# Three reorderings in an attention, MoE and MLP kernel: float64 steps, one expert's sums, and low halves

## The chip, the cores and the metric

The program runs on one core of one Trainium2 chip. Times are device microseconds (us) of one execution. Inputs and outputs are those of the reference; w_in and w_out arrive as float64 and are cut to pairs of float16 by the kernel itself. Below, PE is the matmul engine (PEld its weight loads), DVE the vector engine, ACT the scalar engine, POOL the GpSimd engine and SP the engine that issues the transfers. Each engine works through its own list of instructions in order and waits at an instruction whose inputs or buffers are not ready.

## The reference, cut to what matters

```python
x = attention(q, k, v)                    # (1152, 512): a pooled and a local softmax attention, added
P = sinkhorn(exp(x @ w_gate))             # (1152, 8)
out = 0
for e in range(8):                        # MoE: every token goes through every expert
    h = np.maximum(x @ w1[e], 0.0)        # (1152, 1024)
    out += P[:, e:e + 1] * (h @ w2[e])
h = out @ w_in                            # MoE2: (1152, 2048)
sp = np.where(h > 20.0, h, np.log1p(np.exp(np.minimum(h, 20.0))))
return (h * np.tanh(sp)) @ w_out
```

## The kernel before, in words

Every matrix that goes into a product is split into a float16 high half and a float16 low half, so that a product is three matmuls (high x high, high x low, low x high). The order of the instructions is written out by hand: the Python code issues the products, and between them it calls `tick()`, which takes one step (up to a `yield`) from each of the queues `first` and `second`, and one from `spare` where `more` is true. What a step issues goes to the end of each engine's list at that moment.

**Experts.** Expert 0 is done product by product (L1019), with its second products (`G2`, L1174) at 142 to 175 us. For experts 1 to 7, `G1_7` does the first products with seven block products instead of eight (`SEVEN`). `ORDER7` lists them: 56 words and two dashes, n = 0 to 57, and "2M7" is product M7 of output group 2. A word is six matmuls of 288 columns (L1143). Behind each product stands what empties its bank: ACT copies it out (`snap`, L1105, for M1, M6 and M5; L1160 for M3), or DVE adds it to such a copy (`add`, L1109, for M2, M7 and M4). PE's banks for these products are rings: M7 and M4 share the two banks of ring Z, so that 2M7 (n = 22) must wait until the DVE add of 0M4 (n = 18) is done, 3M7 (n = 24) for that of 1M4 (n = 20), and 4M7 (n = 33) for that of 2M4 (n = 29). M1, M6, M5 and M3 of a group add up in one bank of ring X, so that 4M5 (n = 30) waits for ACT's copy of 4M6 (n = 25), and 0M3 (n = 15) for that of 0M5. Three words after a group's last add ACT writes the ReLU (L1117, "h"), and three words later DVE its low half (L1118, "low").

**Steps beside the first products.** `tick` is called at every odd n and at multiples of 8. `second` carries the split of this expert's w2: four squares for its scale on ACT (L267), then four high parts on ACT (L243, "W") and four low parts on DVE (L256, "wbl"). `spare` carries `Split64.gen`, which turns w_in and w_out into float16 pairs and stores them to DRAM: per piece clamp and shift (DVE L429, L431), join of bits (DVE L434, L436), a square and the next piece's magnitude (ACT L443, L416, on which the next L429 waits), sums and differences of blocks (DVE L487, L534), scaling (ACT L528), and cuts for the store (ACT L492 then DVE L497; ACT L469 then DVE L470). In `G1_7` this queue gets a step where `more` is true, at n = 15, 19, 23, ... 55; in `G2` it gets 24 steps per expert, as it does after the change. It starts near the end of expert 1's first products.

**Sums of W1 of expert 1.** `early_gen` forms three sums of blocks of W1[1] on DVE (L290), their high halves on ACT (L293) and their low halves on DVE (L296), in steps between the last first products of expert 0 (whose results go through ACT L1028, ACT L637 and DVE L1037) and the start of `G2` of expert 0.

**MoE2.** A first product (`First`) goes through `N1` in half steps, i even and i odd, with four of them in flight: a (newest), b, d, e (oldest). `third` and `fourth`, `second2` hold DVE adds that empty PE's banks (L1660), `sums` is one ACT and four DVE instructions (L1663, L1713), `high` one on ACT (L1719), `low` one on DVE (L1722). Half steps alternate with eight-product units of `G2` or of the second products (L1783).

Of the kernel before, what the change touches and what calls it, by code (L numbers as in the profile page):

```python
# [21 lines left out]
def attn_moe_moe2_kernel(ctx: ExitStack, tc: tile.TileContext, q, k, v, w_gate, w1, w2, w_in, w_out, out):  # L22
# [73 lines left out]
    def all_max(m, tag="ma"):  # L96
        ma = sm.tile([128, 1], F32, tag=tag, name=tag)
        nc.gpsimd.partition_all_reduce(ma, m, 128, RED.max)  # L98
        return ma
# [17 lines left out]
    class Steps:  # L117
# [8 lines left out]
        def tick(self, n=1):  # L126
            while n > 0 and self.q:
                try:
                    next(self.q[0])
                    n -= 1  # L130
                except StopIteration:
                    self.q.pop(0)
            return n
# [5 lines left out]
    first, second, spare = Steps(), Steps(), Steps()  # L139
# [139 lines left out]
    class SplitSums(SplitSq):  # L279
# [4 lines left out]
        def early_gen(self, part, halves):  # L284

            (a11, a21), (a12, a22) = [[halves(r)[:, :, n * 512:(n + 1) * 512] for n in range(2)] for r in self.raw]
            s = halves(late["ws"].tile([128, 1024], F32, tag="ws", name="ws"))

            def tt(out, u, v, op):
                nc.vector.tensor_tensor(out=out, in0=u, in1=v, op=op)  # L290

            def hi(n, src):
                nc.scalar.activation(out=halves(part(0, n)), in_=src, func=AF.Copy, scale=self.s)  # L293

            def lo(n, src):
                nc.vector.scalar_tensor_tensor(out=halves(part(1, n)), in0=src, scalar=self.s, in1=halves(part(0, n)),  # L296
                                               op0=ALU.mult, op1=ALU.subtract)

            tt(s, a11, a21, ALU.subtract)
            hi(S3_, s)  # L300
            yield
            tt(a21, a21, a22, ALU.add)
            yield
            lo(S3_, s)
            tt(s, a21, a11, ALU.subtract)
            hi(S2_, s)
            yield
            yield
            lo(S2_, s)
            tt(s, a12, s, ALU.subtract)  # L310
            hi(S4_, s)
            yield
            yield
            lo(S4_, s)
            while not self.free:
                yield
            self.tiles()
            last = None
            for n, src in ((A11_, a11), (A12_, a12), (A22_, a22), (S1_, a21)):
                hi(n, src)  # L320
                yield
                if last:
                    lo(*last)
                yield
                last = n, src
            lo(*last)
            yield
# [59 lines left out]
    class Split64:  # L387
# [21 lines left out]
        def gen(self):  # L409
            for i in range(3):  # L410
                self.fetch(i)

            def magnitude(i):

                w = self.w32()
                nc.scalar.activation(out=w, in_=self.words[i][:, :, 1].bitcast(F32), func=AF.Abs)  # L416
                return w

            last, prev = None, None
            for _ in range(4):  # L420
                yield
            nxt = magnitude(0)
            yield
            for i, (src, f) in enumerate(self.todo):
                w = nxt
                wi = w.bitcast(I32)
                lo, hi = self.words[i][:, :, 0], self.words[i][:, :, 1]

                nc.vector.tensor_scalar(out=w, in0=w, scalar1=LOW, scalar2=HIGH, op0=ALU.max, op1=ALU.min)  # L429

                nc.vector.tensor_scalar(out=wi, in0=wi, scalar1=3, scalar2=2 ** 30 - 1, op0=ALU.logical_shift_left,  # L431
                                        op1=ALU.bitwise_and)
                yield
                nc.vector.scalar_tensor_tensor(out=wi, in0=lo, scalar=29, in1=wi, op0=ALU.logical_shift_right,  # L434
                                               op1=ALU.bitwise_or)
                nc.vector.scalar_tensor_tensor(out=wi, in0=hi, scalar=-2 ** 30, in1=wi, op0=ALU.bitwise_and,  # L436
                                               op1=ALU.bitwise_or)
                self.fetch(i + 3)
                yield
                if f < 8:  # L440
                    mq = sm.tile([128, 2], F32, tag="m6", name="m6")
                b = cvp[0].tile([128, CW], BF16, tag="junk", name="junk", bufs=1)
                nc.scalar.activation(out=b, in_=w, func=AF.Square, accum_out=mq[:, f // 8:f // 8 + 1])  # L443
                if i + 1 < len(self.todo):
                    nxt = magnitude(i + 1)
                if f >= 8:
                    yield
                    m1 = sm.tile([128, 1], F32, tag="m7", name="m7")
                    nc.vector.tensor_tensor(out=m1, in0=mq[:, 0:1], in1=mq[:, 1:2], op=ALU.add)
                    if not src:  # L450
                        m1 = all_max(m1, "ma6")
                    yield
                if last:
                    yield from self.parts_in(*last)
                    last = None
                if f < 8:
                    prev = w
                elif src == 0:
                    last = f - 8, prev, w, m1
                else:  # L460
                    yield from self.parts_out(f - 8, prev, w, m1)
# [626 lines left out]
    def G1_7(w, h, fill):  # L1088
# [32 lines left out]
        def due(n):  # L1121
            lows.sort(key=lambda x: x[0])
            while lows and lows[0][0] <= n:
                lows.pop(0)[1]()

        for n, word in enumerate(ORDER7.split()):
# [3 lines left out]
            else:  # L1130
                gi, m = item
                b, f = gi // 4, gi % 4
                g = open_.setdefault(gi, {})
                a, bn, bank, before = SEVEN[m]
# [30 lines left out]
                    parts(n, b, f + 4, g["r2"])  # L1165
            due(n)
            if n % 2 or n % 8 == 0:
                tick(more=n > 12 and n % 4 == 3)
        due(1000)

    def G2_products(ps, w, h, t, ft):
# [119 lines left out]
    with tc.manual_schedule():  # L1291
# [437 lines left out]
        def N1(c, i, more=True):  # L1729

            if i % 2 == 0:
                if more:
                    n = 8 * c + i // 2
                    for k in range(2):
                        win_load(k, n + 2)
                    firsts.append(First(c, i // 2))
                    firsts[-1].begin()
                else:  # L1740
                    firsts.append(None)
                firsts.pop(0)
            a, b, d, e = firsts[::-1]
            if i % 2 == 0:
                for it, step in ((b, "third"), (a, "begin2"), (d, "sums"), (e, "low")):
                    if it:
                        getattr(it, step)()
            else:
                for it, step in ((a, "second"), (b, "fourth"), (a, "second2"), (d, "high")):
                    if it:  # L1750
                        getattr(it, step)()

# [74 lines left out]
        e = E - 1  # L1827
# [28 lines left out]
        n = [0]  # L1856
# [27 lines left out]
        for c in range(NC2):  # L1884
            n = [0]
# [49 lines left out]
```

## Time and profile before

| | |
|---|---|
| three runs, us | 986.39 median (982.49 to 990.14) |
| profiled execution, us | 983.91 |
| its span, us | 982.1 |
| granted clock of PE, mean | 0.998 of full speed |
| busy share of the span | PE 97%, PEld 66%, DVE 73%, ACT 58%, POOL 7% |
| DMA queue 1 | 122.59 MB, 39.9% of 16 engines' span |

The table's shares are means over the whole program. Attention fills the first 75 us or so, expert 0 ends at 175 us, the first products of experts 1 to 7 begin at about 175, 264, 356, 445, 533, 624 and 712 us and take some 43 us each, the rest of each expert is second products, and MoE2 takes the time from 776 us on.

### The profile page before, as it was taken

Reading aid. Unit: us, or ns where it says so; the run is one execution under the profiler, and the core shown is the slowest. Engines: PE = TensorE matmul, PEld = TensorE weight load, DVE = VectorE, ACT = ScalarE, POOL = GpSimd, SP = SyncE. Lnnn points to the kernel's source line nnn. Section 1 sums busy time; section 2 is a strip of 40 time slices with the busy share of each in tenths; the row PEclk is TensorE's granted clock in tenths of the full one; section 3 lists DMA queues with packets and bytes.
Section 4 is the critical chain, followed back from the end, with each engine's and each line's share of the span. In section 5 each row is a group of like instructions: output and inputs, shape, how many; then the busy total and the mean of one; then the engine's idle time right before and its main releaser. Section 6 shows DMA issues by size and latency. Waiting matters only on the chain. (4 is left out here: it accounts for less than half of the span.)

```text
span 982.1 us, 20942 instructions
## 1 busy us (share of the span) xinstructions
PE 952.6 (97%) x8501; PEld 652.6 (66%) x8504; DVE 716.4 (73%) x1507; ACT 568.2 (58%) x1162; POOL 64.2 (7%) x116
## 2 busy tenths in 40 slices
PE   6899998999999999999999999999999999999998
PEld 5676674774566467547745764674476577999997
DVE  5887578679577949794996789498858467877741
ACT  4776344766376457747763774577375265665631
POOL 5524100000000000000000000000000000000000
PEclk9999999999999999999999999999999999999999
DMA  9863202022413242242424232332303756767781
GB/s 212 166 147 109 90 1 86 1 86 72 161 66 111 69 157 84 106 139 70 151 81 150 87 107 87 134 134 65 124 1 108 288 185 203 264 206 208 224 269 36
DMA packets 97707, 123.91 MB, mean 126 GB/s; under 512 B 36812, under 2 KB 72012, under 8 KB 96588
## 3 DMA queue, kind: packets, MB, share of 16 engines
q1 hardware_dynamic: 97612, 122.59, 39.9%
q8 instruction: 66, 1.08, 0.5%
q14 instruction: 29, 0.24, 0.1%
HBM read 104.48 MB, written 18.09 MB: 125 GB/s over the span
## 5 line engine op out<-in xcount | busy, mean ns | idle before, releaser
L1174 PE MATMUL mm<-wbh,h 128*128 128x512 f16 x1152 | 352.4, 379 | 2.5 <-ACT h L637 2.4
L1174 PEld LDWEIGHTS <-h 128*128 128x128 f16 x1728 | 167.6, 98 | 194.9 <-ACT h L637 2.9
L1174 PE MATMUL mm<-wbl,h 128*128 128x512 f16 x576 | 218.3, 379 | 0.0
L1109 DVE SCALAR_TENSOR_TENSOR r<-mm,s 128x288 f32<-128x288 f32 x168 | 75.5, 455 | 78.3 <-PE mm L1143 73.7
L1143 PE MATMUL mm<-x,wah 128*128 128x288 f16 x672 | 128.8, 287 | 0.0
L1143 PEld LDWEIGHTS <-wx 128*128 128x128 f16 x1008 | 98.9, 98 | 34.0 <-issue 8.9
L1143 PEld LDWEIGHTS <-wah 128*128 128x128 f16 x896 | 88.0, 98 | 27.3 <-issue 1.0
L1143 PE MATMUL mm<-xt,wx 128*128 128x288 f16 x672 | 97.0, 286 | 7.6 <-DVE r L1109 7.6
L1105 ACT ACTIVATE s<-mm 128x288 f32<-128x288 f32 x168 | 66.5, 411 | 61.4 <-PE mm L1143 61.0
L1649 PEld LDWEIGHTS <-win 128*128 128x128 f16 x1536 | 92.3, 98 | 10.2 <-issue 3.9
L1143 PE MATMUL mm<-x,wal 128*128 128x288 f16 x336 | 96.6, 287 | 0.0
L1118 DVE SCALAR_TENSOR_TENSOR h<-r,h 128x576 f16<-128x576 f32 x112 | 81.6, 750 | 0.0
L1117 ACT ACTIVATE h<-r 128x576 f16<-128x576 f32 x112 | 74.3, 680 | 9.4 <-DVE r L1109 9.1
L443 ACT ACTIVATE junk<-w 128x512 bf16<-128x512 f32 x32 | 20.1, 627 | 76.6 <-DVE w L436 74.1
L1207 DVE SCALAR_TENSOR_TENSOR acc<-mm,pc,acc 128x512 f32<-128x512 f32 x63 | 46.8, 746 | 19.6 <-PE mm L1174 19.6
L1656 ACT ACTIVATE s<-mm 128x128 f32<-128x128 f32 x96 | 26.6, 277 | 57.0 <-PE mm L1649 55.6
L98 POOL PARTITION_ALL_REDUCE ma<-m x25 | 14.1, 563 | 670.2 <-DVE m L271 395.6
L1649 PE MATMUL mm<-xc,win 128*128 128x128 f16 x864 | 56.1, 219 | 1.2 <-DVE acc L1207 0.7
L267 ACT ACTIVATE junk<-raw 128x1024 bf16<-128x1024 f32 x52 | 54.9, 1056 | 0.2
L1143 PEld LDWEIGHTS <-wal 128*128 128x128 f16 x448 | 43.9, 98 | 11.2
L1143 PE MATMUL mm<-x,wx 128*128 128x288 f16 x336 | 51.1, 289 | 0.0
L1660 DVE TENSOR_TENSOR tt<-mm,s 128x128 f32<-128x128 f32 x96 | 24.8, 285 | 34.2 <-ACT s L1656 31.9
(287 smaller groups left out, 1543.0 us busy)
## 6 DMA issues: line engine op xcount, KB each, us to landing
raw<-in_moe_w_dram SPq DMA_DIRECT2D x44, 512.0 KB, 4.8
win<-scri SPq DMA_DIRECT2D x40, 512.0 KB, 4.6
win<-scri SPq DMA_DIRECT2D x40, 384.0 KB, 3.7
raw<-in_moe_w_dram SPq DMA_DIRECT2D x10, 1024.0 KB, 5.9
f<-in_moe_w_in_dram SPq DMA_DIRECT2D x16, 512.0 KB, 3.7
f<-in_moe_w_out_dram SPq DMA_DIRECT2D x16, 512.0 KB, 3.6
scr<-st SPq DMA_DIRECT2D x32, 256.0 KB, 2.6
scri<-st SPq DMA_DIRECT2D x56, 128.0 KB, 1.9
```

Of the source, the lines that this page charges most:

```text
L267: nc.scalar.activation(out=junk, in_=r[:, c * 1024:(c + 1) * 1024], func=AF.Square, accum_out=mx[:, 2 * i + c:2 * i + c + 1])
L443: nc.scalar.activation(out=b, in_=w, func=AF.Square, accum_out=mq[:, f // 8:f // 8 + 1])
L1105: nc.scalar.activation(out=t, in_=ps, func=AF.Copy, scale=HSC)
L1109: nc.vector.scalar_tensor_tensor(out=out, in0=ps, scalar=HSC, in1=r, op0=ALU.mult, op1=ALU.add)
L1117: lows.append((n + 3, lambda: nc.scalar.activation(out=hi, in_=r, func=AF.Relu)))
L1118: lows.append((n + 6, lambda: nc.vector.scalar_tensor_tensor(out=lo, in0=r, scalar=0.0, in1=hi, op0=ALU.max, op1=ALU.subtract)))
L1143: nc.tensor.matmul(ps, lhsT=w.part(wi, a)[:, c:c + 128], rhs=factor(b, bn, xi, i), start=(not before and k == 0), stop=(k == 5), skip_grou ...
L1174: nc.tensor.matmul(ps, lhsT=h[ft][:, hi, t * 128:(t + 1) * 128], rhs=wt[:, ws], start=(ft == 0 and n == 0), stop=(ft == FT - 1 and n == 2))
L1207: nc.vector.scalar_tensor_tensor(out=a, in0=ps, scalar=pc[:, t:t + 1], in1=a, op0=ALU.mult, op1=ALU.add)
L1649: nc.tensor.matmul(self.bank(bank), lhsT=self.win[i][:, n, wi, kk * 128:(kk + 1) * 128], rhs=self.x[:, xi, xn, kk * 128:(kk + 1) * 128], s ...
L1656: nc.scalar.activation(out=t, in_=self.ps[:, 0], func=AF.Copy)
L1660: nc.vector.tensor_tensor(out=self.tt[:, o], in0=self.bank(bank), in1=r, op=ALU.add)
```

## The change

Three edits of order; no instruction of the computation is added or taken away.

```diff
@@ early_gen (sums of W1 of expert 1)
             tt(s, a11, a21, ALU.subtract)
+            yield
             hi(S3_, s)
-            yield
             tt(a21, a21, a22, ALU.add)
             yield
             lo(S3_, s)
             tt(s, a21, a11, ALU.subtract)
+            yield
             hi(S2_, s)
-            yield
             yield
             lo(S2_, s)
             tt(s, a12, s, ALU.subtract)
+            yield
             hi(S4_, s)
-            yield
             yield
             lo(S4_, s)
@@ Split64.gen
             last, prev = None, None
-            for _ in range(4):
+            for _ in range(3):
                 yield
@@ G1_7
             if n % 2 or n % 8 == 0:
-                tick(more=n > 12 and n % 4 == 3)
+                tick(more=n % 2 and (n < 24 and n % 6 != 1 or n > 44 and n % 4 == 3))
@@ N1
             if i % 2 == 0:
-                for it, step in ((b, "third"), (a, "begin2"), (d, "sums"), (e, "low")):
+                for it, step in ((b, "third"), (a, "begin2"), (d, "sums")):
                     if it:
                         getattr(it, step)()
             else:
-                for it, step in ((a, "second"), (b, "fourth"), (a, "second2"), (d, "high")):
+                for it, step in ((a, "second"), (b, "fourth"), (a, "second2"), (d, "high"), (e, "low")):
```

In `early_gen` each high half goes to ACT one step after the DVE instruction that forms its input, and no longer in the same step. In `G1_7` the float64 queue still gets 11 steps per expert, now at n = 3, 5, 9, 11, 15, 17, 21 and 23 and then at 47, 51 and 55: none at 25 to 45. In expert 1 the queue starts too late for the early ones; it stands two steps further back from there on, and its last step still falls into expert 7's first products. In `N1` the low half of the oldest product is cut at the end of the odd half step, behind that half step's adds, and no longer at the end of the even one. PE's list of instructions is the same before and after, apart from the numbers of buffers.

Three places of the order, as it stood and as it stands. The first is ACT's list at the end of expert 0's first products: L1028 takes a product of expert 0 out of its bank, L637 makes its high half, and L293 is a high half of a sum of W1[1], whose input `ws` or `raw` DVE forms. Before:

```order
L1028 ACTIVATE r<-mm_2583 128x288
L293 ACTIVATE wx<-ws,sc_w_1_2200 128x1024
L1028 ACTIVATE r<-mm_2605 128x288
L637 ACTIVATE h<-r 128x576
L1028 ACTIVATE r<-mm_2632 128x288
L293 ACTIVATE wx<-ws,sc_w_1_2200 128x1024
L1028 ACTIVATE r<-mm_2650 128x288
L637 ACTIVATE h<-r 128x576
L293 ACTIVATE wx<-ws,sc_w_1_2200 128x1024
L293 ACTIVATE wah<-raw,sc_w_1_2200 128x1024
```

After:

```order
L1028 ACTIVATE r<-mm_2583 128x288
L1028 ACTIVATE r<-mm_2604 128x288
L637 ACTIVATE h<-r 128x576
L293 ACTIVATE wx<-ws,sc_w_1_2200 128x1024
L1028 ACTIVATE r<-mm_2632 128x288
L1028 ACTIVATE r<-mm_2649 128x288
L637 ACTIVATE h<-r 128x576
L293 ACTIVATE wx<-ws,sc_w_1_2200 128x1024 x2
```

Each of the three L293 on `ws` has moved behind the next L1028 and L637 of expert 0. DVE's list is the same in this stretch.

The second place is DVE's list in the first products of expert 7, from the add of 1M4 (n = 20) on: L1109 are the adds of 1M4, 2M7 (n = 22), 3M7 (n = 24) and 3M2 (n = 27) in this order, L534 and L470 are float64 steps. Before:

```order
L1109 SCALAR_TENSOR_TENSOR r<-mm_8748,s_8688 128x288
L1118 SCALAR_TENSOR_TENSOR h<-r,h 128x576
L1109 SCALAR_TENSOR_TENSOR r<-mm_8839,s_8763 128x288
L1118 SCALAR_TENSOR_TENSOR h<-r,h 128x576
L256 SCALAR_TENSOR_TENSOR wbl<-raw,sc_w_7_8772,wbh 128x1024
L534 TENSOR_TENSOR w_8859<-w_8400 128x256
L534 TENSOR_TENSOR w_8859<-w_8467,w_8859 128x256
L1109 SCALAR_TENSOR_TENSOR r<-mm_8862,s_8854 128x288
L1118 SCALAR_TENSOR_TENSOR h<-r,h 128x576
L256 SCALAR_TENSOR_TENSOR wbl<-raw,sc_w_7_8772,wbh 128x1024
L1118 SCALAR_TENSOR_TENSOR h<-r,h 128x576
L1109 SCALAR_TENSOR_TENSOR r<-mm_8893,s_8670 128x288
```

After:

```order
L1109 SCALAR_TENSOR_TENSOR r<-mm_8753,s_8686 128x288
L1118 SCALAR_TENSOR_TENSOR h<-r,h 128x576
L470 TENSOR_TENSOR st<-w_8447,st 128x2x256
L1109 SCALAR_TENSOR_TENSOR r<-mm_8846,s_8768 128x288
L1118 SCALAR_TENSOR_TENSOR h<-r,h 128x576
L256 SCALAR_TENSOR_TENSOR wbl<-raw,sc_w_7_8777,wbh 128x1024
L534 TENSOR_TENSOR w_8447<-w_8489,w_8804 128x256
L534 TENSOR_TENSOR w_8447<-w_8489,w_8447 128x256
L470 TENSOR_TENSOR st<-w_8489,st 128x2x256
L1109 SCALAR_TENSOR_TENSOR r<-mm_8872,s_8861 128x288
```

The cut L470, which stood behind the add of 3M2, now stands ahead of the add of 2M7, a second one ahead of the add of 3M7; from there to the add of 3M4 (n = 31) no float64 row is left.

The third place is DVE's list in MoE2 beside the transposition of the second chunk (L1568, L1570, L1572, L1573) and the end of a tile of second products (L1207). Before:

```order
L1713 TENSOR_TENSOR tt<-tt 128x128 x4
L1722 SCALAR_TENSOR_TENSOR g<-tt,cf_9343,g 128x896
L1568 SCALAR_TENSOR_TENSOR xb<-mm_9714,xcs_9494,xa 128x256
L1570 TENSOR_SCALAR xb<-mm_9714,xcs_9494 128x256
L1207 SCALAR_TENSOR_TENSOR acc<-mm_9547,pc_9176,acc 128x512
L1660 TENSOR_TENSOR tt<-mm_9598,s_9647 128x128
L1660 TENSOR_TENSOR tt<-mm_9677,s_9691 128x128
L1572 TENSOR_TENSOR xb<-xb 128x256
```

After:

```order
L1713 TENSOR_TENSOR tt<-tt 128x128 x4
L1568 SCALAR_TENSOR_TENSOR xb<-mm_9713,xcs_9494,xa 128x256
L1570 TENSOR_SCALAR xb<-mm_9713,xcs_9494 128x256
L1207 SCALAR_TENSOR_TENSOR acc<-mm_9547,pc_9176,acc 128x512
L1660 TENSOR_TENSOR tt<-mm_9598,s_9646 128x128
L1660 TENSOR_TENSOR tt<-mm_9677,s_9691 128x128
L1722 SCALAR_TENSOR_TENSOR g<-tt,cf_9343,g 128x896
L1572 TENSOR_TENSOR xb<-xb 128x256
```

The low half L1722 has moved from ahead of the adds L1660 to behind them.

## Rows read from the trace of the kernel before

**Rows 1.** The page, busy us of each engine, share of the span, instructions

```profile
PE 952.6 (97%) x8501; PEld 652.6 (66%) x8504; DVE 716.4 (73%) x1507; ACT 568.2 (58%) x1162; POOL 64.2 (7%) x116
```

**Rows 2.** PE's waits: engine, tile, line, releaser: us in total, times, longest us

```profile
PE mm L1143 <- DVE r L1109: 7.6, 7, 2.3
...
PE mm L1174 <- ACT h L637: 2.4, 1, 2.4
PE mm L1649 <- DVE tt L1660: 1.9, 3, 0.8
...
PE mm L1649 <- DVE acc L1207: 0.7, 1, 0.7
PE cp L1284 <- DVE cs L1279: 0.7, 1, 0.7
...
PE mm L1143 <- ACT s L1105: 0.4, 2, 0.2
```

**Rows 3.** Timeline of PE, products 4M7: start, us, instruction, [idle before]

```profile
290.63 0.90 PE L1143 MATMUL mm<-xt,wx 128*128 128x288 f16 x6 [2.28 <-DVE r L1109]
...
737.73 0.90 PE L1143 MATMUL mm<-xt,wx 128*128 128x288 f16 x6 [0.64 <-DVE r L1109]
...
739.19 0.90 PE L1143 MATMUL mm<-x,wx 128*128 128x288 f16 x6
```

**Rows 4.** Windows: us, PE, PEld, DVE, ACT, POOL busy, clock, DMA, GB/s

```profile
292.00:294.00 2.00, 2.00 (x11) 1.28 (x9) 2.00 (x5) 1.03 (x3) 0.00 (x0) 0.50 1.06 370
294.00:296.00 2.00, 2.00 (x13) 1.37 (x12) 2.00 (x5) 0.76 (x2) 0.45 (x1) 0.67 0.99 383
150.00:155.00 5.00, 4.16 (x21) 1.86 (x20) 4.79 (x10) 2.01 (x2) 0.00 (x0) 1.00 0.00 0
```

**Rows 5.** Timeline of ACT, then PE, at the sums of W1[1]

```profile
147.55 1.15 ACT L293 ACTIVATE wx<-ws,sc_w 128x1024 f16<-128x1024 f32 x1 [5.61 <-DVE ws L290]
...
149.76 0.39 PE L1174 MATMUL mm<-wbh,h 128*128 128x512 f16 x1 [2.36 <-ACT h L637]
```

**Rows 6.** Timeline of DVE in the first products of expert 7

```profile
729.55 0.46 DVE L1109 SCALAR_TENSOR_TENSOR r<-mm,s 128x288 f32<-128x288 f32 x1 [0.35 <-PE mm L1143]
...
731.89 0.42 DVE L534 TENSOR_TENSOR w<-w 128x256 f32<-128x256 f32 x1
...
732.69 0.45 DVE L1109 SCALAR_TENSOR_TENSOR r<-mm,s 128x288 f32<-128x288 f32 x1
...
736.62 0.69 DVE L470 TENSOR_TENSOR st<-w,st 128x512 f16<-128x512 f32 x1
737.22 0.45 DVE L1109 SCALAR_TENSOR_TENSOR r<-mm,s 128x288 f32<-128x288 f32 x1
```

**Rows 7.** Timelines of ACT and DVE in expert 4, of ACT in expert 7

```profile
462.48 1.14 ACT L243 ACTIVATE wbh<-raw,sc_w 128x1024 f16<-128x1024 f32 x1
...
464.38 1.32 ACT L528 ACTIVATE w<-w,s_out 128x512 f32<-128x512 f32 x2
...
464.57 0.45 DVE L1109 SCALAR_TENSOR_TENSOR r<-mm,s 128x288 f32<-128x288 f32 x1
...
730.75 1.14 ACT L243 ACTIVATE wbh<-raw,sc_w 128x1024 f16<-128x1024 f32 x1
...
735.89 0.64 ACT L469 ACTIVATE st<-w 128x512 f16<-128x512 f32 x1
```

**Rows 8.** Timeline of DVE in the first products of expert 2

```profile
284.06 0.43 DVE L429 TENSOR_SCALAR w<-w 128x512 f32<-128x512 f32 x1 [1.03 <-ACT w L416]
...
284.86 0.45 DVE L1109 SCALAR_TENSOR_TENSOR r<-mm,s 128x288 f32<-128x288 f32 x1
```

**Rows 9.** Groups by line: count | busy us, mean ns | idle before

```profile
L434 DVE SCALAR_TENSOR_TENSOR w<-f,w 128x512 int32<-128x512 int32 x32 | 22.0, 687 | 0.3
```

**Rows 10.** Timeline of DVE, then PE, in MoE2

```profile
823.90 1.15 DVE L1722 SCALAR_TENSOR_TENSOR g<-tt,cf,g 128x896 f16<-128x896 f32 x1
...
826.87 0.83 PE L1649 MATMUL mm<-xd,win 128*128 128x128 f16 x12 [0.81 <-DVE tt L1660]
```

## The prediction

> **What bounds the kernel now.** I read the busy shares first: PE is busy for 97% of the span and DVE for 73% [rows 1]. A change of order on DVE and ACT can therefore gain only where PE stands still, so I read the list of PE's waits next. Those that the three edits can reach are few: 7.6 us in seven waits of first products for a DVE add (L1109) and 0.4 us for ACT copies, 2.4 us in one wait of expert 0's second products for a high half (L637), 0.7 us of a copy that feeds the next one, 1.9 us in three waits of MoE2 for the adds L1660, and 0.7 us for L1207 [rows 2]. Together that is 13.7 us of 982.1. The timeline of PE says where: the long waits of the experts all stand at the product 4M7, 2.28 us in expert 2 and 0.64 us in expert 7 [rows 3]. Last I read the clock. After the 2.28 us wait it is 0.50 for one window of 2 us and 0.67 for the next [rows 4], which costs (1 - 0.50) x 2 + (1 - 0.67) x 2 = 1.66 us on top. So the three edits play for 15.4 us at most.
>
> **Edit 1, sums of W1[1].** ACT came to L293 at 147.55 - 5.61 = 141.94 and waited there for a DVE sum [rows 5]. Behind it in the same list stood L1028 and L637, which PE needed, so PE waited 2.36 us at 149.76. After the edit L1028 and L637 stand ahead of that L293, and their input is a finished product. Those 2.4 us go. Of the 0.7 us of the copy L1284, whose input comes from the same crowded stretch of DVE, I take 0.4, since DVE's list there does not change (bounds 0 and 0.7). What becomes late is the split of W1[1], by one step; PE's first use of it is at 175 us. Edit 1: **-2.8** (-2.4 to -3.1).
>
> **Edit 2, the float64 steps.** No instruction is removed. Steps leave n = 25 to 45, where they stood ahead of the adds that 4M7 needs, and go to n = 3 to 23, where most adds are not waited for. With a product every 0.73 us (739.19 - 737.73 is two of them [rows 3]) I walked through each expert's lists as they will stand. In expert 7 the spare of DVE ahead of 4M7 can be read: two L534 and an L470 stand there, 2 x 0.42 + 0.69 = 1.53 us [rows 6], and PE waits 0.64, so about 0.9 us of foreign work fits for nothing.
>
> Expert 7: the cut L470 that now stands ahead of the add of 2M7 needs ACT's L469, which stands right behind ACT's second W. That W began at 730.75; L528 (1.3 us) no longer stands between the first and the second W, so W begins earlier, though by about 1.0 only, since the copy ahead of it then waits for its product. W takes 1.14 and L469 0.64 [rows 7]: L469 ends near 731.4 and L470 near 732.0, where the add of 2M7 stood at 729.55. From there to the add of 2M4 DVE has the same rows as before (two L534, one L470) and had no idle time, so the lateness of 2.45 reaches 4M7: 2.45 + 0.64 = 3.1, part of it shown at 3M4.
>
> Expert 4: L528 now stands ahead of the second W, and L469 and L470 come at n = 23. From W's start to L528's start is 1.90 in the rows, W with a copy and a ReLU row. So W begins at 462.48 + 1.32, L469 at 465.70, L470 at 466.34 and the add of 3M7 at 467.0, where it stood at 464.57 [rows 7]: 2.5 late, less the two L534 (0.84) that no longer follow it, 1.6 at 4M7.
>
> Expert 2: before, L429 waited 1.03 us for ACT's magnitude L416, the add behind it stood still until 284.86 [rows 8], and that made the 2.28 us. The same step now comes at n = 17, ahead of the add of 0M4, for which 2M7 waits. Ahead of that magnitude ACT has a W (1.14 alone, 1.90 with a copy and a ReLU row [rows 7]), then the square and the magnitude (about 1.3, an estimate from the L528 pair, as large), and L429 and L431 take 0.80 (284.06 to 284.86): the add starts 3.2 to 4.0 us after product 17 ends, where 0.7 would do. It may be 1.7 late for nothing (three products of 0.73, less 0.51 from add to PE, 737.22 to 737.73 [rows 3, 6]), so 2M7 waits 0.8 to 1.6; I take 1.2 (outer bounds 0 and 2.3, the whole of the old wait). At n = 21 L434 and L436 (2 x 0.69 [rows 9]) add 1.4 - 0.9 = 0.5 at 4M7.
>
> Experts 3, 5 and 6 have such a pair at n = 15 to 23 too: 0.5 each at 4M7, and 0.3 in all for 0M3, which waits for ACT copies while steps crowd ACT at n = 3 to 15. Expert 1 keeps its 0.2. Sum after: 3.1 + 1.6 + 1.7 + 1.8 + 0.2 = 8.4, against 7.6 + 0.4 before: **+0.4** (bounds -7.8 with no hold at all, +10.8 with all six like expert 7).
>
> [...] Without any such hold in experts 2, 4 and 7, edit 2 would give -4.9 and not +0.4.
>
> The clock: the 2.28 us wait lost 1.66 us, but the clock is 1.00 from 150 to 155 us although a 2.36 us wait stood in front [rows 4, 5]. Expert 7's wait, split in two, may do either. I count half: **-0.8** (0 and -1.7).
>
> [...] The two waits of this trace, alike in length, ended at 0.50 and at 1.00. By the one the forecast is 0.8 higher, by the other 0.8 lower.
>
> The transfers of the moved steps (fetch and store of a piece on SP) move with them, and this expert's weight loads stand behind them; no wait of PE in the list is for a transfer, and the pieces are all stored by the end of expert 7's first products, as before. I cost that at nothing; a weight quarter that came late would cost PE its wait directly.
>
> **Edit 3, low halves.** Before 826.87 DVE cut a low half (L1722, 1.15 us) at 823.90, and then the adds L1660 came, for which PE waited 0.81 [rows 10]. With the low half behind them these 0.81 go, and so does one more of the three, whose adds also have a low half and nothing that waits for PE ahead (0.55, half of the 1.1 that is left of 1.9). The third, and L1207's 0.7, wait for a row that is itself waiting for PE, so nothing is gained there. The low half is used by second products half a step or more later. **-1.4** (0 to -2.6).
>
> **Sum.** -2.8 + 0.4 - 0.8 - 1.4 = -4.6. The profiled execution took 983.9, so 979.3; the runs' median is 986.4, 2.5 above it, and against that I forecast **981.8**.
>
> **The rivals.** (a) All waits go, as the places of the steps suggest: nothing at n = 25 to 45, so 4M7 waits nowhere. For it: the waits before are behind such steps. Against it: experts 2, 4 and 7 as walked through. All 13.7 + 1.7 = 15.4 go: **971.0**. (b) The holds are more than I found: two more experts hold as expert 4 does (1.6 with a clock drop of 1.7, for 0.5 each), and no drop is saved. 981.8 + 2 x 2.8 + 0.8 = **988.2**, no change. For it: ACT gets two steps more before n = 24 beside squares, W and copies; against it: most of those steps have their inputs ready by a word or two. (c) Slower: in each of the six experts 2 to 7 DVE stands behind ACT as in expert 7, 3.1 + 1.7 of clock = 4.8 each. 28.8 + 0.2 - 8.0 - 1.7 - 2.8 - 1.4 = +15.1: **1001.5**. It decides from 4.0 us per expert on, since 9.9 us (1%) + 13.7 us of gains are 23.6. Against it: L470 behind a W stands only in experts 4 and 7.
>
> **How the numbers follow.** My forecast 0.60 (its own range 978 to 985, from the bounds of edits 1 and 3, the clock, and 2 us either way on the holds), (a) 0.13, (b) 0.22, (c) 0.05. The range 973 to 989 leaves out (c), the half of (a) below 973 and the third of (b) above 989: 0.05 + 0.07 + 0.07. One per cent, 9.9 us, is about what a measurement of this kernel can tell from no change. Faster by more than that, below 976.5, is (a) and a hundredth of the forecast: 0.14. Slower is (c): 0.05. The rest, 0.81, is within 1%.
>
> **What would show it.** PE's list of waits without L1174 on L637 (edit 1). MoE2 with one L1660 wait left, near 0.5 (edit 3). In the experts: waits of 3 us in expert 7 at 3M4 and 4M7 with L470 waiting for L469 in front; one near 1.2 at 2M7 in expert 2 with L429 waiting for L416; one near 1.6 at 4M7 in expert 4. The forecast is wrong if these waits are not there (a), if 2M7 or 3M7 wait in further experts (b, c), or if the windows behind the waits show a clock of 0.50 more than once.

## The result, and the profile after

The changed kernel took 976.7 us in the median (975.4 to 977.9) against 987.1 for the kernel before: a ratio of 0.990, 95% interval 0.986 to 0.994. Beside two more series of the kernel before the ratio was 0.991 (0.988 to 0.994) and 0.993 (0.990 to 0.996). Over all 22 executions of the changed kernel and the 63 of the kernel before in the three later series the medians are 976.8 and 985.4, the means 978.1 and 986.3: some 8.2 us less, 0.8%. Its profiled execution took 975.4 us, with a span of 973.6.

The page's busy shares of the kernel after:

```profile
PE 953.0 (98%) x8504; PEld 652.9 (67%) x8504; DVE 717.0 (74%) x1507; ACT 568.0 (58%) x1162; POOL 61.1 (6%) x116
```

PE's busy time is that of before within 0.4 us [rows 1], and the span is 8.5 us shorter: PE stands still for less time, and does nothing faster. From PE's list of waits (engine, tile, line, releaser: us in total, times, longest):

```profile
PE mm L1143 <- DVE r L1109: 5.9, 7, 2.3
...
PE mm L1143 <- ACT s L1105: 0.8, 2, 0.6
...
PE cp L1284 <- DVE cs L1279: 0.7, 1, 0.7
```

L1174 on L637, L1660 and L1207 [rows 2] are gone from the list. The first products still wait: 6.7 us for DVE adds and ACT copies, where it was 8.0. The timeline of PE shows where they wait now (start, us, instruction, idle time before it and what ended it):

```profile
276.80 0.90 PE L1143 MATMUL mm<-xt,wx 128*128 128x288 f16 x6 [1.07 <-DVE r L1109]
...
285.69 0.90 PE L1143 MATMUL mm<-xt,wx 128*128 128x288 f16 x6 [0.50 <-DVE r L1109]
...
460.32 0.41 PE L1143 MATMUL mm<-xt,wah 128*128 128x288 f16 x2 [0.58 <-ACT s L1105]
...
463.44 0.77 PE L1143 MATMUL mm<-xt,wx 128*128 128x288 f16 x5 [0.75 <-DVE r L1109]
...
543.93 0.90 PE L1143 MATMUL mm<-xt,wx 128*128 128x288 f16 x6 [0.64 <-DVE r L1109]
...
727.67 0.40 PE L1143 MATMUL mm<-x,wah 128*128 128x288 f16 x2 [0.40 <-DVE r L1109]
...
731.60 1.58 PE L1143 MATMUL mm<-xt,wx 128*128 128x288 f16 x6 [2.30 <-DVE r L1109]
```

276.80 is 2M7 of expert 2 and 285.69 its 4M7; 460.32 and 463.44 are 4M5 and 4M7 of expert 4; 543.93 is 2M7 of expert 5; 727.67 and 731.60 are 3M4 and 4M7 of expert 7. Expert 2's 2.28 us [rows 3] has become 1.07 and 0.50, and expert 7's 0.64 has become 0.40 and 2.30.

PE's list of instructions is the same in both kernels, so the same matmul can be found in both traces, and how much earlier it starts can be followed along the program. The steps of this difference give each edit's share (a step counts the whole delay, also what the list of waits leaves out):

| place | edit | forecast, us | steps in the two traces, us |
|---|---|---|---|
| up to 76 us: the attention and the first products of expert 0 beside it | none | 0 | -1.4 |
| second products of expert 0 | 1 | -2.8 | -2.5 - 0.35 = -2.9 |
| expert 2 | 2 | -0.7 | +1.2 - 0.2 - 1.8 = -0.7 |
| expert 3 | 2 | -0.9 | +0.4 - 1.5 = -1.1 |
| expert 4 | 2 | +1.4 | +0.4 + 0.9 = +1.3 |
| expert 5 | 2 | -1.6 | +0.8 - 0.6 - 1.9 = -1.7 |
| expert 6 | 2 | -0.2 | +0.3 + 0.2 - 0.7 = -0.2 |
| expert 7 | 2 | +2.5 | +0.6 + 1.7 = +2.2 |
| a clock drop in expert 2, one in expert 7 | 2 | -0.8 | -1.7 + 1.7 = 0 |
| MoE2 | 3 | -1.4 | -0.9 - 0.2 - 1.0 - 0.2 - 0.6 - 0.8 - 0.3 = -4.0 |

The forecast of an expert is its wait in the sum less the one it had (for experts 3, 5 and 6 the 0.6 each that the prediction gave them). The edits come to -2.9 - 0.2 - 4.0 = -7.1 us; the other 1.4 of the 8.5 lie ahead of 76 us, in rows that no edit touches.

### The profile page after: what moved, and what is told of

Its sections match the earlier page's. It is cut to its first block, busy times and chain, and to the rows that moved or that the text cites. A ratio compares the mean times of both kernels' runs of the same rounds, so it can differ in the third digit from the quotient of the medians.

```text
span 973.6 us, 20982 instructions
## 1 busy us (share of the span) xinstructions
PE 953.0 (98%) x8504; PEld 652.9 (67%) x8504; DVE 717.0 (74%) x1507; ACT 568.0 (58%) x1162; POOL 61.1 (6%) x116
## 5 line engine op out<-in xcount | busy, mean ns | idle before, releaser
L1174 PE MATMUL mm<-wbh,h 128*128 128x512 f16 x1152 | 352.2, 379 | 0.0
L1174 PEld LDWEIGHTS <-h 128*128 128x128 f16 x1728 | 167.8, 98 | 191.8 <-issue 0.4
L1174 PE MATMUL mm<-wbl,h 128*128 128x512 f16 x576 | 218.3, 379 | 0.0
L1143 PE MATMUL mm<-x,wah 128*128 128x288 f16 x672 | 128.7, 287 | 0.4 <-DVE r L1109 0.4
L1109 DVE SCALAR_TENSOR_TENSOR r<-mm,s 128x288 f32<-128x288 f32 x168 | 75.2, 453 | 64.8 <-PE mm L1143 59.5
L1143 PEld LDWEIGHTS <-wx 128*128 128x128 f16 x1008 | 99.0, 98 | 32.7 <-issue 7.4
L1143 PEld LDWEIGHTS <-wah 128*128 128x128 f16 x896 | 87.8, 98 | 28.5 <-issue 2.4
L1143 PE MATMUL mm<-xt,wx 128*128 128x288 f16 x672 | 97.7, 287 | 5.6 <-DVE r L1109 5.5
L1143 PE MATMUL mm<-x,wal 128*128 128x288 f16 x336 | 96.4, 287 | 0.0
L1118 DVE SCALAR_TENSOR_TENSOR h<-r,h 128x576 f16<-128x576 f32 x112 | 81.0, 748 | 0.6 <-ACT h L1117 0.6
L1207 DVE SCALAR_TENSOR_TENSOR acc<-mm,pc,acc 128x512 f32<-128x512 f32 x63 | 46.8, 745 | 21.4 <-PE mm L1174 21.4
L98 POOL PARTITION_ALL_REDUCE ma<-m x25 | 10.9, 439 | 664.9 <-DVE m L271 413.9
L1143 PEld LDWEIGHTS <-wal 128*128 128x128 f16 x448 | 43.9, 98 | 11.2
L1143 PE MATMUL mm<-x,wx 128*128 128x288 f16 x336 | 50.6, 287 | 0.1
L1019 PE MATMUL mm<-x,wah 128*128 128x288 f16 x256 | 47.7, 286 | 0.0
```

Source lines behind the costliest of these rows:

```text
L1019: nc.tensor.matmul(self.ps, lhsT=wt[:, ws], rhs=x[:, xi, kk, o:o + CH], start=(n == 0), stop=(n == 3 * KT - 1))
L1109: nc.vector.scalar_tensor_tensor(out=out, in0=ps, scalar=HSC, in1=r, op0=ALU.mult, op1=ALU.add)
L1118: lows.append((n + 6, lambda: nc.vector.scalar_tensor_tensor(out=lo, in0=r, scalar=0.0, in1=hi, op0=ALU.max, op1=ALU.subtract)))
L1143: nc.tensor.matmul(ps, lhsT=w.part(wi, a)[:, c:c + 128], rhs=factor(b, bn, xi, i), start=(not before and k == 0), stop=(k == 5), skip_grou ...
L1174: nc.tensor.matmul(ps, lhsT=h[ft][:, hi, t * 128:(t + 1) * 128], rhs=wt[:, ws], start=(ft == 0 and n == 0), stop=(ft == FT - 1 and n == 2))
L1207: nc.vector.scalar_tensor_tensor(out=a, in0=ps, scalar=pc[:, t:t + 1], in1=a, op0=ALU.mult, op1=ALU.add)
```

## The experiments

**Each edit alone.** These kernels hold one of the three edits of the diff, unchanged, and nothing else of it.

> Only edit 1 (the sums of W1[1]) is made. Theory: the traces of before and after differ at 149 us by the wait of L1174 for L637, 2.36 us with 0.19 us behind it, and by nothing else in that stretch: this kernel shows no wait there, the wait of 0.7 us at L1284 stays, and it takes 2.5 us less than before. Rival: the measured 10.4 us between before and after is more than the three edits' waits add up to (2.5 + 1.3 + 2.7 = 6.5), so one of the edits is worth more than its waits. If it is this one, it takes 4 us or more off.

> Only edit 2 (the float64 steps) is made. Theory: the waits of first products go from 8.0 us to about 6.7 (1.1 at 2M7 and 0.5 at 4M7 in expert 2, 0.6 and 0.75 in expert 4, 0.6 in expert 5, 0.4 and 2.3 in expert 7), and the clock drop moves from expert 2 to expert 7 at the same price of 1.7 us: 1.3 us less than before. The 2.4 us wait for L637 and the MoE2 waits of 2.65 us are as before. Rival: the edit is worth 4 to 5 us, by something that is not in PE's list of waits.

> Only edit 3 (MoE2's low halves) is made. Theory: all four waits of MoE2 (0.71, 0.81, 0.45 and 0.68 us) go, also the one that the profile puts down to L1207, since the low half of 1.15 us stood ahead on DVE in each: 2.65 us less than before, and the waits of the first products as before. Rival, from the prediction: only two of the four go, 1.4 us. The attention's first 50 us are the same instructions as before; if they again take some 1.5 us less in this profile than in before's, that part of the difference is scatter between executions and no edit's.

> The changed kernel once more, on the chip on which the three edits run alone. Theory: the three edits' gains add up to it, 6.5 us by the waits. Rival: it is some 10 us below before here too, which the waits do not cover; then the rest is either in one of the edits or in before's own scatter (982.5 to 990.1 so far).

| kernel | median, us | ratio to before | steps from 76 us on, without clock drops |
|---|---|---|---|
| edit 1 alone | 984.9 | 0.999 (0.996 to 1.001) | -2.9 |
| edit 2 alone | 985.4 | 1.000 (0.997 to 1.002) | -0.2 |
| edit 3 alone | 981.3 | 0.996 (0.994 to 0.999) | -4.0 |
| all three | 976.5 | 0.991 (0.988 to 0.994) | -7.1 |
| before | 985.2 | | |

The steps of each edit alone stand at the same places and have the same size, to 0.02 us, as in the kernel with all three: the edits add up and do not touch each other. The times say less, because executions of one kernel scatter by 10 us (the 63 of before went from 981.2 to 992.0). Edit 1's median is only 0.4 us below that of before, where its theory had 2.5; the interval holds 0 as well as 2.9, so its share rests on the traces. In the profiles most of the scatter lies ahead of expert 1: a copy L1284, which starts at 154.5 in before, starts at 160.3 with edit 2 alone, and at 150.2 and 152.8 in two profiles of the changed kernel, where edit 1 accounts for 2.9, though the rows of the attention are the same in all. Windows of the kernel with edit 2 alone (us; busy of PE, PEld, DVE, ACT, POOL; clock; DMA, GB/s):

```profile
26.00:28.00 2.00, 2.00 (x15) 1.63 (x15) 1.45 (x5) 0.26 (x2) 0.00 (x0) 0.50 0.59 126
46.00:48.00 2.00, 2.00 (x20) 1.26 (x20) 1.80 (x3) 0.29 (x1) 0.00 (x0) 0.50 0.49 98
56.00:58.00 2.00, 2.00 (x72) 1.62 (x71) 1.74 (x5) 1.65 (x4) 0.05 (x1) 0.50 0.92 165
```

The clock is 0.50 at 26 us, and again in each window from 46 to 58 us. No window of the attention fell below 1.00 in the profile of before or in the first profile of after. So the rival falls: no edit is worth more than 4.0, and of the first 10.4 us some 3 stand in no step of an edit. But the theory's sizes, taken from the list of waits, were wrong too. A wait that came or went here delayed PE by 0.16 us more than the list says (1.24 for the 1.07 at 2M7 of expert 2). The list counts from the end of the last matmul, and matmuls overlap in these traces: the L1174 at 799.97 below is 0.38 us long, and the next matmul starts 0.22 us after it began. Delays of 0.1 to 0.3 us thus stood in no wait at all. Edit 2 is worth 0.2 and not 1.3. Both lists have eight waits beside the one of expert 1 that stays, so there the 0.16 cancel, but the edit brings delays that are not listed: 0.1 and 0.15 in expert 2, 0.15 at 4M7 of expert 3, and 0.29, 0.23 and 0.29 at 0M3, 4M5 and 4M7 of expert 6. Edit 3 is worth 4.0, and not the 2.65 of its four waits. This shows on DVE and PE. DVE before, ahead of the product at 801.00:

```profile
797.41 1.02 DVE L1713 TENSOR_TENSOR tt<-tt 128x128 f32<-128x128 f32 x4 [0.21 <-ACT tt L1663]
798.35 1.15 DVE L1722 SCALAR_TENSOR_TENSOR g<-tt,cf,g 128x896 f16<-128x896 f32 x1
799.42 0.48 DVE L1568 SCALAR_TENSOR_TENSOR xb<-mm,xcs,xa 128x256 f32<-128x256 f32 x1
799.81 0.47 DVE L1570 TENSOR_SCALAR xb<-mm,xcs 128x256 f32<-128x256 f32 x1
800.20 0.74 DVE L1207 SCALAR_TENSOR_TENSOR acc<-mm,pc,acc 128x512 f32<-128x512 f32 x1
800.86 0.48 DVE L1660 TENSOR_TENSOR tt<-mm,s 128x128 f32<-128x128 f32 x2
```

From 797.41 to L1660 DVE has no idle time, so L1207 waited for nobody: it was late by the low half at 798.35. PE in the kernel before, at that product and at a later one:

```profile
799.91 0.38 PE L1174 MATMUL mm<-wbh,h 128*128 128x512 f16 x1
801.00 1.50 PE L1649 MATMUL mm<-xc,win 128*128 128x128 f16 x24 [0.71 <-DVE acc L1207]
...
810.87 1.71 PE L1649 MATMUL mm<-xc,win 128*128 128x128 f16 x24
```

The kernel with edit 3 alone, DVE:

```profile
798.41 0.47 DVE L1568 SCALAR_TENSOR_TENSOR xb<-mm,xcs,xa 128x256 f32<-128x256 f32 x1
...
799.20 0.74 DVE L1207 SCALAR_TENSOR_TENSOR acc<-mm,pc,acc 128x512 f32<-128x512 f32 x1
799.86 0.47 DVE L1660 TENSOR_TENSOR tt<-mm,s 128x128 f32<-128x128 f32 x2
800.25 1.14 DVE L1722 SCALAR_TENSOR_TENSOR g<-tt,cf,g 128x896 f16<-128x896 f32 x1
```

and PE at the same two products:

```profile
799.97 0.38 PE L1174 MATMUL mm<-wbh,h 128*128 128x512 f16 x1
800.19 1.50 PE L1649 MATMUL mm<-xc,win 128*128 128x128 f16 x24
...
810.06 1.50 PE L1649 MATMUL mm<-xc,win 128*128 128x128 f16 x24
```

The add L1660 now follows at 799.86, with L1722 behind it. From the last L1174 to the product's start it was 801.00 - 799.91 = 1.09 and is 800.19 - 799.97 = 0.22: 0.87 less, where the list of waits had 0.71. And the 24 matmuls that took 1.71 us at 810.87 take 1.50: that delay of 0.21 us stood in no wait. Two more of 0.23 and 0.30 are like it. (In the kernel before PE's idle time there, from the end of one matmul to the start of the next, is only 0.05 to 0.13 us.)

**Edit 2 left out, and the changed kernel once more.**

> Edits 1 and 3 without edit 2: the float64 steps stand where they stood before. Theory: edit 2 is worth 0.2 us in the traces, so this kernel takes the same time as the changed one within 1 us, with 8.0 us of waits in first products where that has 6.7. Rival: edit 2 carries 2 us or more of the gain, and this kernel is that much slower than the changed one.

> The changed kernel a third time. From the first product of expert 0 on its PE rows took 7.1 us less than before's in both profiles, outside clock drops. Its 10 runs so far had a mean granted clock of 0.9966, those of before 0.994, although the drops fall into the first 120 us, where both kernels hold the same instructions. Theory: that was chance, and more runs come to a clock near 0.994 and a time 7 to 8 us below before's. Rival: the changed kernel keeps the higher clock and is 9 to 10 us below.

Without edit 2 the median was 980.1 (ratio 0.995, 0.992 to 0.998), beside 977.1 for the changed kernel (0.993, 0.990 to 0.996) in the same series. That is 3.0 us apart, where the theory had 1 at most and the rival 2 or more. By the steps from 76 us on the two differ by 0.2 us outside clock drops (the third profile of the changed kernel has a delay of 0.2 us in MoE2 that its first two do not have, and is level with it); the profile without edit 2 has two more clock drops, at 124 and 298 us, which cost 1.7 us each (clocks of 0.61 and 0.54, and of 0.63 and 0.52, in two windows of 2 us). The intervals of the two times overlap, and edit 2 alone had taken nothing off, so a share of edit 2 in the time is not shown. The changed kernel's mean clock in these 12 executions was 0.993, that of before over its 63 is 0.994, and its median was 7.7 us below before's: the theory held, and the 0.997 of the first 10 did not come again. In executions with a mean clock of 0.995 and more the means are 984.5 (35 of before) and 976.4 (18 of after), 8.1 us apart; why that is 1 us more than the 7.1 of the traces stays open.

**The holds.** Does DVE stand behind ACT in experts 7, 4 and 2, or is it only full, with its own rows one behind the other and no wait between them? DVE in expert 7's first products, in the changed kernel:

```profile
723.05 0.69 DVE L470 TENSOR_TENSOR st<-w,st 128x512 f16<-128x512 f32 x1 [2.18 <-ACT st L469]
723.67 0.45 DVE L1109 SCALAR_TENSOR_TENSOR r<-mm,s 128x288 f32<-128x288 f32 x1
```

and ACT there:

```profile
721.37 1.14 ACT L243 ACTIVATE wbh<-raw,sc_w 128x1024 f16<-128x1024 f32 x1
722.41 0.62 ACT L469 ACTIVATE st<-w 128x512 f16<-128x512 f32 x1
```

DVE waits 2.18 us at L470 for L469, which stands behind the W of 721.37, and the add of 2M7 comes at 723.67. In expert 4 the same pair has a much shorter wait:

```profile
458.40 0.69 DVE L470 TENSOR_TENSOR st<-w,st 128x512 f16<-128x512 f32 x1 [0.39 <-ACT st L469]
```

In expert 2 it is L429, which waits for the magnitude L416:

```profile
275.50 0.43 DVE L429 TENSOR_SCALAR w<-w 128x512 f32<-128x512 f32 x1 [0.98 <-ACT w L416]
275.96 0.43 DVE L431 TENSOR_SCALAR w<-w 128x512 int32<-128x512 int32 x1
276.30 0.81 DVE L1109 SCALAR_TENSOR_TENSOR r<-mm,s 128x288 f32<-128x288 f32 x2
```

Three kernels take these apart. In the first, the high part of each cut is issued one step ahead of its low part:

```diff
             sub(t[:, hw:CW], b[:, hw:CW], t[:, 0:hw])
+            p = high(a)
             yield
-            store(0, a)
-            yield
+            store(0, p)
+            p = high(b)
             sub(a[:, 0:hw], b[:, 0:hw], t[:, hw:CW])
             sub(a[:, hw:CW], b[:, hw:CW], a[:, hw:CW])
-            store(2, b)
             yield
-            store(4, t)
+            store(2, p)
+            p = high(t)
             yield
-            store(6, a)
+            store(4, p)
+            p = high(a)
+            yield
+            store(6, p)
             yield
```

(`high` is ACT's half of `cut`, and `store` now begins with DVE's half.)

> The changed kernel, with the cuts of w_out's pieces (L469, L470) taken apart: ACT's half of a cut goes out one step ahead of DVE's half, in the same number of steps. No instruction is added. Theory (DVE stands behind ACT): the waits of 0.4 and 2.3 us of expert 7 at 3M4 and 4M7 go, and so does expert 4's 0.75 us at 4M7; the rest of the first products' waits stays; 3.5 us less than the changed kernel, and no clock drop behind 4M7 of expert 7 (1.7 us more where the drop was). Rival (DVE is simply too full there, with two L534, two L470 and the low parts ahead of the adds): the waits of experts 7 and 4 stay within 0.5 us, and the time with them.

Its median was 973.7 (ratio to before 0.988, 0.985 to 0.991). DVE's cuts (now L544) in expert 7 wait no longer:

```profile
722.27 0.68 DVE L544 TENSOR_TENSOR st<-w,st 128x512 f16<-128x512 f32 x1
...
725.89 0.68 DVE L544 TENSOR_TENSOR st<-w,st 128x512 f16<-128x512 f32 x1
```

PE, at 4M5 of expert 4 and at 4M5 and 4M7 of expert 7 (L1143 is L1155 here):

```profile
462.35 0.40 PE L1155 MATMUL mm<-xt,wah 128*128 128x288 f16 x2 [1.10 <-ACT s L1117]
...
728.21 0.41 PE L1155 MATMUL mm<-xt,wah 128*128 128x288 f16 x2 [0.45 <-ACT s L1117]
...
730.93 0.90 PE L1155 MATMUL mm<-xt,wx 128*128 128x288 f16 x6 [0.35 <-DVE r L1121]
```

4M7 of expert 7 waits 0.35 instead of 2.30, and 3M4 not at all: there the holds were the cause. In expert 4 the theory failed: 4M7 waits 0.55, where it was 0.75, and DVE's rows ahead of it, from 456.42 on, follow each other without a wait. There DVE is mostly full, as the rival has it; one wait of 0.61 us stands before that stretch, of L1118 for the ReLU on ACT, which taking the cuts apart does not touch. (2M7 of expert 5, which the theory did not name, waits 0.23 instead of 0.64.) And 4M5 of expert 7 now waits 0.45 for an ACT copy, and that of expert 4 waits 1.10 instead of 0.58. ACT in expert 4 shows why:

```profile
457.34 1.15 ACT L243 ACTIVATE wbh<-raw,sc_w 128x1024 f16<-128x1024 f32 x1
458.38 0.62 ACT L539 ACTIVATE st<-w 128x512 f16<-128x512 f32 x1
...
459.76 0.63 ACT L539 ACTIVATE st<-w 128x512 f16<-128x512 f32 x1
...
460.85 1.15 ACT L243 ACTIVATE wbh<-raw,sc_w 128x1024 f16<-128x1024 f32 x1
```

Two L539 (the former L469) stand between two W, where one stood, and the copy comes later by its 0.5 us. In all 1.9 us are gained by the steps and not 3.5. The theory has the cause in expert 7, the rival in expert 4, and a part of the gain is given back on the other engine; 0.4 us more is lost in MoE2, behind a wait of 0.23 us for a transfer of w_in, which the profile with both edits below does not show. In the second kernel a piece's magnitude goes out a step earlier:

```diff
                 self.fetch(i + 3)
+                if i + 1 < len(self.todo):
+                    nxt = magnitude(i + 1)
                 yield
...
                 nc.scalar.activation(out=b, in_=w, func=AF.Square, accum_out=mq[:, f // 8:f // 8 + 1])
-                if i + 1 < len(self.todo):
-                    nxt = magnitude(i + 1)
```

> The changed kernel, with a piece's magnitude (L416 on ACT) issued one step ahead of the clamp and shift (L429, L431 on DVE) that wait for it. Theory: the 1.07 us wait at 2M7 of expert 2 goes, the waits of experts 4 and 7 stay as in the changed kernel: 1.1 us less than it. Rival: the add of 0M4 is late by DVE's own work, and the wait stays.

DVE at the same place of expert 2:

```profile
279.70 0.45 DVE L1109 SCALAR_TENSOR_TENSOR r<-mm,s 128x288 f32<-128x288 f32 x1
280.07 0.42 DVE L429 TENSOR_SCALAR w<-w 128x512 f32<-128x512 f32 x1
...
280.87 0.81 DVE L1109 SCALAR_TENSOR_TENSOR r<-mm,s 128x288 f32<-128x288 f32 x2
```

L429 starts without a wait and 2M7 with it; the steps show -1.06 at 2M7, and -0.56 in expert 5, where the same hold had made the 0.64 us; the 0.50 at 4M7 of expert 2 has become 0.49 at 4M5. Expert 7 waits 0.40 and 2.30 as in the changed kernel. The median was 978.1 (0.990, 0.988 to 0.993): the 1.6 us do not show above the scatter.

> Both of these edits together. Theory: first products wait 2.1 us in all instead of 6.7 (0.2 in expert 1, 0.5 at 4M7 in expert 2, 0.2 in expert 3, 0.6 in expert 4, 0.6 in expert 5), 4.6 us less than the changed kernel, and 1.7 us more where that had the clock drop in expert 7: 970 to 972 us. Rival: the steps that no longer wait push work onto adds that did not wait so far, and half of it comes back.

Both together: 975.2 in the median (0.988, 0.985 to 0.990), above the theory's 970 to 972, the lowest execution 970.4, and by the steps 3.7 us less than the changed kernel. First products wait 3.5 us in all, with 1.10 at 4M5 of expert 4 the largest; waits for ACT copies grew from 0.8 to 2.4. A fifth of the expected 4.6 did not come, and not half, as the rival had it. By the steps this kernel beats the kernels with one of the two edits; by the time it beats only the kernel before. The changed kernel did not run in this series (before: 986.7), so no time tells these kernels from it or from each other: the one with the cuts alone has the lower median, 973.7.

**Another place for the steps.**

```diff
-                tick(more=n % 2 and (n < 24 and n % 6 != 1 or n > 44 and n % 4 == 3))
+                tick(more=n % 2 and (2 < n < 16 or n in (47, 49, 51, 55)))
```

> The changed kernel with the float64 steps of the first products at n = 3, 5, 7, 9, 11, 13, 15 and 47, 49, 51, 55, so none from 17 to 45, and nothing else changed. Theory: the holds of experts 2, 4 and 7 came with the steps at n = 17, 21 and 23; they go, and only short waits for ACT copies around n = 15 are left: about 5 us less than the changed kernel by the waits. Rival: with seven steps one after the other ACT and DVE are late by n = 15 already, 0M3 and the products of ring Z (0M4 at n = 18, 2M7) wait a microsecond or more in several experts, and the time is the same or longer.

The median was 975.7 (0.990, 0.987 to 0.993), and the steps give 2.5 us less than the changed kernel. PE's list of waits:

```profile
PE mm L1143 <- ACT s L1105: 3.3, 7, 0.8
...
PE mm L1143 <- ACT r L1160: 1.2, 1, 1.2
```

All holds of DVE are gone (0.2 us are left in expert 1), and 4.5 us of waits for ACT copies are there instead, 1.18 at one place of expert 5. Half of the theory's gain holds, and half of the rival's objection does: ACT is late where the steps are packed, but only that one wait is over a microsecond.

**Holds in the old places.** Edits 1 and 3, with both of the edits to the cuts and the magnitude, and the float64 steps at n = 15, 19, ... 55 as before.

> Edits 1 and 3, the float64 steps where they stood before, and the two edits that take DVE from behind ACT (cuts taken apart, magnitude a step earlier). Theory: of the old waits only expert 2's 2.28 us came from such a hold; the others (1.5, 1.75, 0.8, 0.6 us at 4M7) come from DVE being full between the adds of 2M7 and 2M4 and stay. So 2 us less than edits 1 and 3 alone, and 1.5 to 2 us more than the changed kernel with the same two edits. Rival: the holds made all of the old waits, and this kernel is as fast as that one or faster.

The median was 974.8 (0.989, 0.985 to 0.993). By the steps it is 1.7 us below the changed kernel, 1.9 below edits 1 and 3 alone and 2.0 above the changed kernel with the same two edits. 4M7 of experts 2, 3, 5 and 7:

```profile
288.24 0.90 PE L1155 MATMUL mm<-xt,wx 128*128 128x288 f16 x6 [1.30 <-DVE r L1121]
...
377.64 0.90 PE L1155 MATMUL mm<-xt,wx 128*128 128x288 f16 x6 [1.46 <-DVE r L1121]
...
554.43 0.90 PE L1155 MATMUL mm<-xt,wx 128*128 128x288 f16 x6 [0.52 <-DVE r L1121]
...
732.78 0.90 PE L1155 MATMUL mm<-xt,wx 128*128 128x288 f16 x6 [0.91 <-DVE r L1121]
```

Expert 2 still waits 1.30 of its 2.28 us, although the magnitude for L429 goes out a step earlier: the hold had made 1.0, and for the rest DVE is full; in the kernel before none of its rows waits from 284.52, behind L429, to the add at 290.12 that 4M7 needs. Expert 3 waits 1.46 as before: there DVE is full, in the kernel before without a wait from 373.30 to the add at 381.20. Expert 7 waits 0.91, where it was 0.64, and its 4M5 waits 0.58 for an ACT copy, where it had no wait. The theory's two sums came out, but by other parts: it was wrong on half of expert 2, and on expert 5, where the hold had made most of the 1.75 and which made up for it.

## Why the prediction was right or wrong

The direction held, and the range of 973 to 989 held 976.7. The forecast of 981.8 was 5.1 us too high against the first median, 5.0 against 976.8, and the time lies outside the forecast's own range of 978 to 985.

**Edit 1: right in size, by two errors that cancel.** L1028 and L637 come ahead of L293, and the wait for L637 went. But the 0.4 us of L1284 that I added did not: it still waits 0.7. In its place the two waits of 2.36 and 0.19 were worth 2.52 and 0.35, 0.16 more each than the list shows.

**Edit 2: right to 0.6 us, with the late adds where they were named, but in part by luck.** The forecast was +0.4 for the waits; the steps show -0.2. 2M7 of expert 2 waits 1.07 (forecast 1.2) with L429 behind L416; 4M7 0.50 (0.5); expert 4 waits 0.58 and 0.75 (1.6 in all); expert 7 0.40 and 2.30 (3.1), with L470 behind L469 behind W, and the add of 2M7 2.5 us late. In both of the longer holds DVE's rows behind stood still until ACT was done: for 2.18 us at 723.05, ahead of the add of 2M7, and for 0.98 us at 275.50.

In expert 4 the add of 3M7 was late as forecast: it starts at 459.00, where 464.57 [rows 7] less the 7.7 us that the changed kernel is ahead there would be 456.87, so 2.1 late (forecast 2.5). But only 0.39 of it was a wait for L469, and 0.61 one that the forecast does not have, of L1118 for the ReLU on ACT; the rest is DVE's own rows. With the hold at L470 taken away 4M7 kept 0.55 of its 0.75. The same holds for the reading that L429's wait "made the 2.28 us" of expert 2: without that hold 1.30 is left.

The term that failed is "0.5 each at 4M7" with 0.3 for 0M3, for experts 3, 5 and 6: expert 6 has no wait of the list left (and delays of 0.29, 0.23 and 0.29 at 0M3, 4M5 and 4M7), expert 3 a wait of 0.23 at 4M5 and an unlisted 0.15 at 4M7, expert 5 one of 0.64, at 2M7 and not 4M7. By the starts of the matmuls these delays come to 2.1 us, where the sum had 1.8: the places were wrong, and that the size is near is luck.

**The clock: the term failed.** "I count half" gave -0.8. The drop of expert 2 [rows 4] went, and one came behind the 2.30 us of expert 7, in the first profile of after:

```profile
732.00:734.00 2.00, 2.00 (x10) 1.24 (x9) 2.00 (x3) 0.95 (x2) 0.00 (x0) 0.50 0.03 8
```

That is 0.50 here, and 0.91 and 0.73 in the windows around it: 1.7 us lost, as before. A second profile of the same kernel, at the same place, behind the same wait of 2.30:

```profile
734.00:736.00 2.00, 1.77 (x15) 1.42 (x15) 2.00 (x4) 1.12 (x3) 0.00 (x0) 1.00 0.03 8
```

The clock is 1.00. With such a wait in expert 7 it fell in three of five profiles, with expert 2's 2.28 in three of four; of the three profiles of the changed kernel itself one has it. So few profiles show no difference between the two places, and a saving of 0.8 us is not shown.

**Edit 3: the mechanism right, the size wrong by 2.6 us, the largest error.** The step that failed is "The third, and L1207's 0.7, wait for a row that is itself waiting for PE". DVE's rows were back to back there, which the timeline of before would have shown. All four waits went, 2.65 us; each was worth 0.16 us more than the list gives it, 0.6 in all; and three delays of 0.21, 0.23 and 0.30 were in no wait. That is 4.0, outside my bound of 2.6, which was the sum of waits in a list.

**The sum's base.** I set -4.6 against the median of three runs, 986.4. By the traces -7.1 would have given 979.3 there, and 978.3 from the median of all runs of before, 985.4. The rest up to 976.8 is the 1 to 1.5 us that stays open: no step of an edit holds it. That the wide range held the time says little for the sum, which missed 2.5 of the 7.1 us.

**The rivals.** (a) did not come: first products wait 6.7 us. (b) and (c) did not: no further expert waits as 4 or 7 do. Faster by more than 1% had 0.14 and within 1% 0.81: the first median is 1.05% below that of before, the medians of all executions are 0.9% apart, so which of the two it is lies within the scatter.

## What to carry to other kernels

A row moved to a free place must find its input ready there (in expert 7 L470 waited 2.18 us for L469, and the add of 2M7 behind it came 2.5 us late): ask which engine forms it, and how many rows stand ahead on that engine; where one step holds both halves of a hand-over between two engines, put them into two steps, and look at what then stands closer together on the first engine (4M5 of expert 4 went from 0.58 to 1.10). Where PE's waits are summed up as the most that an edit can give, add the delays that the list leaves out (0.1 to 0.3 us here) and the 0.16 us that each wait cost here beyond its idle time: in MoE2 the two made half as much again, 4.0 for 2.65. An edit of 4 us in a kernel that scatters by 10 is measured by the starts of the same instructions in two traces, and not by its time.

## What the runs showed of the hardware

The granted clock fell to 0.50 of full speed at places that differ between executions of the same rows: behind a wait of 2.3 us in the experts in six cases of nine, in the attention in some profiles and not in others, and twice in the middle of expert 0, right behind the 80 small matmuls of L1242 (8 or 16 columns, 2.35 us in all): in the kernel without edit 2 and in the kernel with edit 3 alone, whose row is

```profile
118.00:120.00 2.00, 2.00 (x10) 1.25 (x9) 0.00 (x0) 0.41 (x1) 0.00 (x0) 0.50 1.02 393
```

Each drop behind one wait cost 1.7 us by the clock of its windows; with edit 2 alone the attention had one that lasted at 0.50 from 46 to 58 us. The mean clock of an execution went from 0.981 to 1.000, and those of before at 0.986 to 0.988 took some 6 us more than those at 0.998 and above (989.3 to 992.0 against 981.2 to 985.5). Which such wait, and which run of the 80 small matmuls, brings a drop no run here tells.
